# The gathered rows of expert 1: turned on the TensorE, with its weights issued from ScalarE's queue

## The chip, the cores and the metric

The kernel runs on one core of one Trainium2 chip. The metric is the device time of one execution in microseconds (us). The kernel before was timed three times: 347.15, 348.68 and 349.33 us, median 348.68 us. A fourth execution was recorded by the hardware profiler; all times inside the program come from it.

The core has five engines with a queue of instructions each: the TensorE (PE in the profile, its weight loads PEld), VectorE (DVE), ScalarE (ACT), GpSimd (POOL) and SyncE (SP). DMAs are issued from the queues of SP, ACT and POOL, and each engine carries out its own queue in order.

## The reference: what is computed

Two layers follow one another. The first is an mLSTM cell over 4 sequences, 8 heads, 768 steps and heads of 40, which gives a row of 320 numbers for each of the 3072 tokens. The second sends each token to one of eight experts by its id and applies that expert's two matrices:

```python
expert_idx = token_ids * np.int64(2654435761) % np.int64(E)      # E = 8
for e in range(E):
    mask = expert_idx == e
    xe = x[mask]                                                  # some 384 rows of 320
    h = np.maximum(xe @ w1[e], 0.0)                               # w1[e]: 320 x 1024
    out[mask] = h @ w2[e]                                         # w2[e]: 1024 x 320
```

All of it is fp32.

## The kernel before

**First half.** The sequence is cut into 24 pieces of 128 steps, which are worked through one after the other (the loop at L877). The rows that come out are stored to `x_rows` in DRAM. Beside this the routing is worked out: `g_idx` holds for each expert the numbers of its rows in `x_rows`, `s_idx` where the results go. Near the end of this half, 256 rows of expert 0 are gathered, turned on the TensorE (`early_turn`, L782) and put through layer 1 (L985), since they come from pieces that are done early.

**An expert's rows.** Each expert has CAP = 416 places: NJ = 3 blocks of 128 rows and RM = 32 more. The 32 of four experts are gathered together in one block of 128 (`xr0` for experts 0 to 3). Layer 1 needs the rows turned: `xT` has the 320 features along the partitions, as three blocks of 128, the third of which has only 64 features and carries them twice, for a product that uses both halves of the array. A row block is gathered by an indirect DMA from POOL (`gather`, L111).

There are two ways from gathered rows to `xT`:

- By way of slots in DRAM (experts 1 to 7): `fetch(e)` (L1198) gathers three blocks into `xg` and stores them to `x_slots` (L1206), `blocks(e)` (L1215) reads them back with 12 DMAs in pieces of 32 features, 128 bytes each, and `turned(e)` (L1223) turns all 32 x 32 squares with one VectorE instruction (L1225). The stores and the reads are issued by SP, and each waits for the one before it to land.
- On the TensorE (the rest of expert 0): `turn` (L1010) makes two transposes into PSUM, copies the last 64 features beside themselves on VectorE (L1015), makes the third transpose (L1016) and copies the result to `xT` on VectorE (L1020) or ScalarE (L1018). `turn_third` does so for the third block of expert 0, `turn_rest` for `xr0`, of which only the first 32 columns, those of expert 0, are kept.

**An expert's products.** Expert 0 uses plain products (`layer1`, L144, and `layer2`, L1122). Experts 1 to 7 use a scheme of seven products of half size in place of eight (`layer1_by_seven`, `layer2_by_seven`); it needs sums of blocks of the weights and of the rows beforehand: `sums_of_w1` (four VectorE instructions, L1029 to L1032) gives `sw`, `sums_of_x` (four, L1036 to L1039) gives `tx`, `differences_of_w2` (four on GpSimd) gives `tw`. The first product of an expert needs `w1t` and `xT`; the second needs `sw` and `tx`. The third row block and the 32 rows use plain products.

**Weights.** `weights` (L92) issues four DMAs: `w1t` (1024 KB, L98), `w1c` in two of 128 KB each (L101) and `w2t` (1280 KB, L103). In PSUM, `psum()` hands out eight banks in turn.

**The order of the work.** The program's text fixes each engine's order. After the first half it reads: `fetch(0)` (the third block of expert 0 and `xr0`, and the store of `xr0` to the slots, L1213); the first three weight DMAs of expert 1; `fetch(1)`; `blocks(1)`; expert 1's `w2t`; then in the loop (L1246) for expert 0 `fetch(2)`, `blocks(2)`, the weights of expert 2, and its products: layer 2 of two row blocks with `turn_third` after the first and `turn_rest` inside the second, a scatter of each to the output (a copy from PSUM on ScalarE, L997, and an indirect DMA of POOL, L1001), layer 1 of the remaining 160 rows, `sums_of_w1`, `turned(1)`, `sums_of_x`, and layer 2 of the third block. All these weights are issued by SP, so that expert 1's stand in one queue with the stores and reads of the slots.

Of the kernel before, what the change touches and what calls it, by code (L numbers as in the profile page):

```python
# [9 lines left out]
F32 = mybir.dt.float32  # L10
# [8 lines left out]
P = 128  # L19
# [4 lines left out]
def kernel(  # L24
# [24 lines left out]
    nc = tc.nc  # L49
# [4 lines left out]
    Dm = H * D  # L54
    E, _, F = moe_w1.shape
# [9 lines left out]
    DB = len(dch)  # L65

    NJ = 3
    RM = 32
    EG = P // RM
    NM = NJ * P  # L70
    CAP = NM + RM
# [17 lines left out]
    s_idx = consts.tile([P, NC], I32, name="s_idx")  # L89
    xe = consts.tile([1, NX + 1], I32, name="xe")  # L90

    def weights(src1, src2, wpool, w2pool, eng=None, meanwhile=lambda: None):  # L92

        eng = eng or nc.sync
        w1t = wpool.tile([P, 2, F], F32, name="w1t")
        w1c = wpool.tile([P, FB // 2, P], F32, name="w1c")
        w2t = w2pool.tile([P, FB, Dm], F32, name="w2t")
        eng.dma_start(w1t[:], src1[: 2 * P, :].rearrange("(a p) f -> p a f", p=P))  # L98
        last = src1[2 * P :, :].rearrange("d (a two f) -> two d a f", two=2, f=P)
        for i in range(2):  # L100
            eng.dma_start(w1c[i * P // 2 : (i + 1) * P // 2], last[i])  # L101
        meanwhile()
        eng.dma_start(w2t[:], src2.rearrange("(a p) d -> p a d", p=P))  # L103
        return w1t, w1c, w2t

# [5 lines left out]
    def gather(xg, idx, rows=N):  # L111
        nc.gpsimd.indirect_dma_start(  # L112
            out=xg, out_offset=None, in_=x_d[:rows, :], in_offset=bass.IndirectOffsetOnAxis(ap=idx, axis=0),
        )

    W = {}

    def load_weights(e, *args):

        W[e] = weights(moe_w1[e], moe_w2[e], wpools[e % 3 > 0], w2pools[e % 6 > 0], None, *args)  # L120

    def slices_of(e):

# [72 lines left out]
    with tc.tile_pool(name="gates", bufs=1) as gp, \  # L196
# [189 lines left out]
        def turn(s, what, tag="tr"):  # L386
            turned_in(s, what, tag)
            turned_out(s, what)
# [618 lines left out]
            tc.declare_no_dep(ins, group="rows_out", reason="disjoint rows")  # L1007
            tc.add_to_no_dep_group("rows_out", ins)

    def turn(xg, dst, on_act, n=P):  # L1010

        tp = psum().rearrange("p (d c) -> p d c", c=P)[:, :DB]
        for db in range(2):
            nc.tensor.transpose(tp[:, db, :], xg[:, db * P : (db + 1) * P], ident[:])
        nc.vector.tensor_copy(xg[:, Dm:], xg[:, 2 * P : Dm])  # L1015
        nc.tensor.transpose(tp[:, 2, :], xg[:, 2 * P :], ident[:])  # L1016
        if on_act:
            nc.scalar.copy(dst, tp[:, :, :n])  # L1018
        else:
            nc.vector.tensor_copy(dst, tp[:, :, :n])  # L1020

    def bank(i):
        return psum()[:, :CAP]
# [98 lines left out]
    def layer2(w, h, js, idx, apart, between=lambda j: None, within=lambda j, fb: None):  # L1122
        for j in js:
            zp = psum()[:, :Dm]
            for fb in range(FB):
                nc.tensor.matmul(  # L1126
                    zp, lhsT=h[:, fb, j * P : (j + 1) * P], rhs=w[2][:, fb, :],
                    start=(fb == 0), stop=(fb == FB - 1),
                )
                within(j, fb)  # L1130
            scatter(zp, idx(j), apart)
            between(j)
# [57 lines left out]
    def cols_of(t, c0):  # L1190
        return lambda j: t[:, c0 + j : c0 + j + 1]

    with tc.manual_schedule():
        xTs, hrem, xbs = {}, {}, {}
        xr0 = xp.tile([P, DB * P], F32, name="xr0", bufs=1)
        xTs[0] = xT0

        def fetch(e):  # L1198
            if e == 0:
                gather(xg0[:, 2, :Dm], cols_of(g_idx, 0)(2))  # L1200
                gather(xr0[:, :Dm], cols_of(g_idx, NR)(0))
            else:
                xg = xp.tile([P, NJ, Dm], F32, name="xg")
                for j in range(NJ):
                    gather(xg[:, j], cols_of(g_idx, e * NJ)(j))
                nc.sync.dma_start(xs_d[e, :NM].rearrange("(t p) d -> p t d", p=P), xg[:])  # L1206
            if e % EG == 0:
                if e:
                    xr = xp.tile([P, Dm], F32, name="xrg", bufs=1)
                    gather(xr[:], cols_of(g_idx, NR + e // EG)(0))  # L1210
                else:
                    xr = xr0[:, :Dm]
                nc.sync.dma_start(xs_d[e : e + EG, NM:], xr[:])  # L1213

        def blocks(e):  # L1215
            xb = xbs[e] = xp.tile([P, CAP // 32, DB, 32], F32, name="xb")
            rows = xs_d[e].rearrange("(g j) d -> j g d", j=32)
            for q in range(4):
                for c in range(DB):
                    d0 = c * P + (q if c + 1 < DB else q % 2) * 32  # L1220
                    nc.sync.dma_start(xb[q * 32 : (q + 1) * 32, :, c], rows[:, :, d0 : d0 + 32])  # L1221

        def turned(e):  # L1223
            xT = xTs[e] = xp.tile([P, DB, CAP], F32, name="xT")
            nc.vector.transpose(xT.rearrange("p c (g j) -> p g c j", j=32), xbs.pop(e)[:])  # L1225

        def turn_third():
            turn(xg0[:, 2], xT0[:, :, 2 * P : NM], False)

        def turn_rest():  # L1230
            turn(xr0, xT0[:, :, NM:], True, RM)

        def rest(g):
            zp = psum()[:, :Dm]
            for fb in range(FB):
                for i in range(EG):
                    nc.tensor.matmul(  # L1237
                        zp[i * RM : (i + 1) * RM, :], lhsT=hrem[g][:, i, fb, :], rhs=W[g * EG + i][2][:, fb, :],
                        start=(fb == 0), stop=(fb == FB - 1),
                    )  # L1240
            scatter(zp, cols_of(s_idx, NR + g)(0), True)

        fetch(0)
        load_weights(1, lambda: (fetch(1), blocks(1)))
        h = h0
        for e in range(E):  # L1246
            g, i = e // EG, e % EG
            if e + 2 < E:
                fetch(e + 2)
                blocks(e + 2)  # L1250
                load_weights(e + 2)
            if i == 0:
                hrem[g] = xp.tile([P, EG, FB, RM], F32, name="hrem")
            if e == 0:
                layer2(W[0], h, range(2), cols_of(s_idx, 0), True, lambda j: j == 0 and turn_third(), lambda j, fb: (j, fb) == (1, FB - 3) and turn_rest())
                layer1(W[0], xT0, h, 2 * P, CAP, bank)
                sw = sums_of_w1(W[1])
                turned(1)
                tx = sums_of_x(xTs[1])
            else:  # L1260
                tw = differences_of_w2(W[e])
                sh = xp.tile([P, 4, FB // 2, P], F32, name="sh", bufs=1)
                layer1_by_seven(
                    W[e], sw, xTs[e], tx, h, lambda: 2 < e < E - 1 and turned(e + 1),
                    lambda g: sums_of_h(h, sh, g, nc.vector if g else nc.gpsimd),
                )
            nc.gpsimd.tensor_copy(hrem[g][:, i], h[:, :, NM:])
            layer2(W[e], h, (2,), cols_of(s_idx, e * NJ), True)
            if 0 < e < E - 1:
                sw = sums_of_w1(W[e + 1])  # L1270
            if i == EG - 1 and e + 1 < E:
                rest(g)
            if e + 1 == E:
                nc.gpsimd.drain()
            if e > 0:
                txs = []

                def meanwhile():
                    if e < 3:
                        turned(e + 1)  # L1280
                    if e + 1 < E:
                        txs.append(sums_of_x(xTs[e + 1]))

                layer2_by_seven(W[e], tw, h, sh, cols_of(s_idx, e * NJ), meanwhile)
                tx = txs[0] if txs else None
            if e + 1 == E:
                rest(g)
    nx = nc.values_load(xe[0:1, NX : NX + 1], min_val=0, max_val=NX)
    with tc.If(nx > 0):
        with tc.For_i(0, nx, 1) as k:  # L1290
            ex = nc.sync.value_load(xe[0:1, bass.ds(k, 1)], min_val=0, max_val=E - 1)
            gs = xp.tile([P, 2], I32, name="gs")
            nc.vector.tensor_copy(gs[:, 0:1], g_idx[:, bass.ds(k + (NC - NX), 1)])
            nc.vector.tensor_copy(gs[:, 1:2], s_idx[:, bass.ds(k + (NC - NX), 1)])
            w = weights(
                moe_w1[bass.ds(ex, 1)].rearrange("e d f -> (e d) f"),
                moe_w2[bass.ds(ex, 1)].rearrange("e f d -> (e f) d"), wpools[0], w2pools[0],
            )
            xr = xp.tile([P, DB * P], F32, name="xr0", bufs=1)
            xT = xp.tile([P, DB, CAP], F32, name="xT")  # L1300
            gather(xr[:, :Dm], gs[:, 0:1])
            turn(xr, xT[:, :, :P], False)
            layer1(w, xT, h0, 0, P, bank)
            layer2(w, h0, range(1), lambda j: gs[:, 1:2], False)

# [29 lines left out]
```

## Time and profile before

| what | us |
|---|---|
| median of three runs | 348.68 |
| the three runs | 347.15, 348.68, 349.33 |
| the profiled execution | 349.48 |
| its span, first to last instruction | 347.7 |
| TensorE busy in it | 326.8 |
| expert 0's second part begins (layer 2 of the first block) | 133.62 |
| expert 1's first product begins | 158.86 |

The profiled execution is 1.78 us longer than its span, which is what lies before the first and after the last instruction, and 0.80 us longer than the median. In rows of the timeline the columns are the start in us from the span's beginning, the time it took, the engine, the line, the operation, what it writes and reads, how many are merged in the row, and in brackets how long the engine was idle before and what ended that. SPq, ACTq and POOLq are issues of DMAs: their time is that of the issue, not of the transfer.

### The profile page before, as it was taken

Reading aid. Unit: us, or ns where it says so; the run is one execution under the profiler, and the core shown is the slowest. Engines: PE = TensorE matmul, PEld = TensorE weight load, DVE = VectorE, ACT = ScalarE, POOL = GpSimd, SP = SyncE. Lnnn points to the kernel's source line nnn. Section 1 sums busy time; section 2 is a strip of 40 time slices with the busy share of each in tenths; the row PEclk is TensorE's granted clock in tenths of the full one; section 3 lists DMA queues with packets and bytes.
Section 4 is the critical chain, followed back from the end, with each engine's and each line's share of the span. In section 5 each row is a group of like instructions: output and inputs, shape, how many; then the busy total and the mean of one; then the engine's idle time right before and its main releaser. Section 6 shows DMA issues by size and latency. Waiting matters only on the chain.

```text
span 347.7 us, 10269 instructions
## 1 busy us (share of the span) xinstructions
PE 326.8 (94%) x4059; PEld 289.8 (83%) x4059; DVE 225.3 (65%) x526; ACT 131.7 (38%) x342; POOL 207.0 (60%) x325
## 2 busy tenths in 40 slices
PE   8889979999988799797999999999999999999994
PEld 8668879999977687567899899889989889899892
DVE  7698978888878641046676696834785775764610
ACT  4777567777756421111511411411411501511510
POOL 7795579898753416417625956933954946627613
PEclk9999999999999999999999999999999999999998
DMA  6997989998799984948596967959579478001001
GB/s 125 171 192 131 178 151 162 192 190 181 150 229 219 239 297 90 311 88 286 84 340 142 260 224 175 326 101 289 179 132 310 123 175 240 2 18 41 1 20 41
DMA packets 161977, 59.12 MB, mean 170 GB/s; under 512 B 140389, under 2 KB 157409, under 8 KB 161897
## 3 DMA queue, kind: packets, MB, share of 16 engines
q1 hardware_dynamic: 156694, 47.47, 59.3%
q0 software_dynamic: 3168, 10.49, 9.3%
q8 instruction: 33, 0.54, 0.7%
q10 hardware_dynamic: 2064, 0.48, 0.6%
q14 instruction: 18, 0.14, 0.1%
HBM read 46.25 MB, written 12.33 MB: 168 GB/s over the span
## 4 chain that ended last, share of the span: by engine, by line
PE 72%; DMA 8%; DVE 7%; issue 4%; SPq 3%; POOL 3%; ACT 2%; POOLq 0%; DVEq 0%; ACTq 0%
PE mh L1075 20%; PE mh L1159 15%; PE mh L1126 9%; PE mh L1083 6%; DMA v<-in_v_dram 5%; PE xh L534 5%; PE tr L397 4%; PE sp L461 3%; PE mh L160 2%; DMA x_slots<-xg 2%; DVE w L477 2%; SPq L1221 1%; PE mh L1237 1%; PE ab L420 1%; PE tr L513 1%
## 5 line engine op out<-in xcount | busy, mean ns | idle before, releaser
L1001 POOL DMA_INDIRECT out_dram<-zo,s_idx x26 | 26.5, 1020 | 69.9 <-issue 41.2
L1126 PE MATMUL mh<-w2t,h 128*128 128x320 f32 x160 | 44.9, 432 | 0.0
L1126 PEld LDWEIGHTS mh<-w2t,h 128*128 128x128 f32 x160 | 30.1, 190 | 11.0
L1061 DVE TENSOR_TENSOR h<-u,mh 128x416 f32<-128x416 f32 (+1 forms) x56 | 25.4, 475 | 16.5 <-PE mh L1083 8.4
L112 POOL DMA_INDIRECT xg<-x_rows,g_idx x24 | 23.5, 978 | 16.1 <-issue 6.7
L1075 PE MATMUL mh<-tx,sw 128*128 128x208 f32 x168 | 31.9, 340 | 0.0
L1075 PEld LDWEIGHTS mh<-tx,sw 128*128 128x128 f32 x168 | 29.7, 190 | 0.2 <-DVE tx L1037 0.2
L477 DVE TENSOR_TENSOR w<-sp,w 128x384 f32<-128x384 f32 x48 | 24.4, 550 | 7.0 <-ACT w L424 7.0
L1061 DVE TENSOR_TENSOR u<-m,mh 128x416 f32<-128x416 f32 x28 | 16.5, 588 | 18.8 <-PE mh L1075 15.6
L1159 PE MATMUL mh<-tw,sh 128*128 128x160 f32 x168 | 27.4, 299 | 0.0
L461 PE MATMUL sp<-qT,kT 64*64 64x64 f32 (+1 forms) x960 | 23.7, 233 | 2.8 <-DVE w L477 2.7
L1075 PE MATMUL mh<-xT,w1t 128*128 128x208 f32 x112 | 23.2, 340 | 3.2 <-DVE xT L1225 3.2
L461 PEld LDWEIGHTS sp<-qT,kT 64*64 64x64 f32 x960 | 19.8, 134 | 7.3 <-issue 4.6
L534 PE MATMUL xh<-v,w 128*64 128x41 f32 x384 | 25.9, 228 | 0.0
L534 PEld LDWEIGHTS xh<-v,w 128*64 128x64 f32 x384 | 24.5, 138 | 0.0
L1159 PEld LDWEIGHTS mh<-tw,sh 128*128 128x128 f32 x168 | 24.3, 190 | 0.0
L1075 PEld LDWEIGHTS mh<-xT,w1t 128*128 128x128 f32 x112 | 19.7, 190 | 3.7 <-DVE xT L1225 3.7
L1089 ACT COPY m<-mh 128x416 f32<-128x416 f32 x14 | 7.1, 507 | 40.7 <-PE mh L1075 31.5
L424 ACT ACTIVATE w<-ab 128x384 f32<-128x384 f32 x48 | 21.1, 484 | 2.6 <-PE ab L423 2.4
L1083 PE MATMUL mh<-xT,w1c 64*128 64x208 f32 x224 | 21.6, 342 | 0.0
L1159 PE MATMUL mh<-w2t,h 128*128 128x160 f32 x112 | 21.0, 300 | 0.0
L1083 PEld LDWEIGHTS mh<-xT,w1c 64*128 64x128 f32 x224 | 19.3, 187 | 1.8 <-issue 1.8
(276 smaller groups left out, 826.1 us busy)
## 6 DMA issues: line engine op xcount, KB each, us to landing
w2t<-in_moe_w_dram SPq DMA_DIRECT2D x7, 1280.0 KB
w1t<-in_moe_w_dram SPq DMA_DIRECT2D x7, 1024.0 KB
xb<-x_slots SPq DMA_DIRECT2D x84, 52.0 KB
k<-in_k_dram SPq DMA_DIRECT2D x24, 160.0 KB
v<-in_v_dram SPq DMA_DIRECT2D x24, 160.0 KB
og<-in_o_gate_dram SPq DMA_DIRECT2D x24, 160.0 KB
q<-in_q_dram SPq DMA_DIRECT2D x23, 160.0 KB
x_slots<-xg SPq DMA_DIRECT2D x7, 480.0 KB
```

What stands on the lines that cost most here:

```text
L112: nc.gpsimd.indirect_dma_start(out=xg, out_offset=None, in_=x_d[:rows, :], in_offset=bass.IndirectOffsetOnAxis(ap=idx, axis=0),)
L397: nc.tensor.transpose(tp[:, j, :], d[what][:, 2 * j : 2 * j + 2, :].rearrange("p h d -> p (h d)"), ident[:])
L424: nc.scalar.activation(w[:, hf], ab, AF.Exp)
L461: nc.tensor.matmul(sp[hf][o * HB : (o + 1) * HB, m, bs], lhsT=kT[r, 2 * m + j, i], rhs=qT[r, 2 * m + j, ts], start=True, stop=True,)
L477: nc.vector.tensor_tensor(d["w"][:, hf], d["sp"][hf], d["w"][:, hf], op=ALU.mult)
L534: nc.tensor.matmul(xh[half[i], hs], lhsT=lhsT, rhs=rhs, start=first[i], stop=last, skip_group_check=True)
L1001: ins = nc.gpsimd.indirect_dma_start(out=out[:, :], out_offset=bass.IndirectOffsetOnAxis(ap=idx, axis=0), in_=zo[:], in_offset=None, bound ...
L1061: nc.vector.tensor_tensor(o, a, b, op=ALU.add)
L1075: nc.tensor.matmul(pair(bank[n])[:, a], lhsT=lhsT(g + a), rhs=rhs, start=first and a == 0, stop=True, skip_group_check=True,)
L1083: nc.tensor.matmul(pair(bank[n])[:, a], lhsT=w1c[k, g + a, :], rhs=xT[k, 2, r], start=False, stop=True, skip_group_check=True,)
L1126: nc.tensor.matmul(zp, lhsT=h[:, fb, j * P : (j + 1) * P], rhs=w[2][:, fb, :], start=(fb == 0), stop=(fb == FB - 1),)
L1159: nc.tensor.matmul(bank[n], lhsT=lhsT(f), rhs=rhs(f), start=first and f == 0, stop=f == FB // 2 - 1, skip_group_check=True,)
```

## The change

Three things change, all around expert 1:

1. `fetch(1)` gathers its three blocks into a new tile `xg1` that has room for the doubled features, and no longer stores them to the slots; `blocks(1)` and `turned(1)` are gone. Instead `turn_second(j)` turns each block on the TensorE after expert 0's layer 1; the copies from PSUM go to VectorE, ScalarE and VectorE.
2. `turn_rest` also copies columns 32 to 64 of the turned `xr0` block, which are expert 1's 32 rows, to its `xT`.
3. Expert 1's weights are issued from ScalarE's queue, after ScalarE's copies for the two scatters of expert 0. `fetch(2)`, `blocks(2)` and expert 2's weights come behind the two scatters too, and no longer ahead of them.

```diff
-    def weights(src1, src2, wpool, w2pool, eng=None, meanwhile=lambda: None):
+    def weights(src1, src2, wpool, w2pool, eng=None):
...
-        meanwhile()
         eng.dma_start(w2t[:], src2.rearrange("(a p) d -> p a d", p=P))
...
-    def load_weights(e, *args):
+    def load_weights(e, eng=None):
 
-        W[e] = weights(moe_w1[e], moe_w2[e], wpools[e % 3 > 0], w2pools[e % 6 > 0], None, *args)
+        W[e] = weights(moe_w1[e], moe_w2[e], wpools[e % 3 > 0], w2pools[e % 6 > 0], eng)
...
-    def turn(xg, dst, on_act, n=P):
+    def turn(xg, *dsts):
...
         nc.tensor.transpose(tp[:, 2, :], xg[:, 2 * P :], ident[:])
-        if on_act:
-            nc.scalar.copy(dst, tp[:, :, :n])
-        else:
-            nc.vector.tensor_copy(dst, tp[:, :, :n])
+        for i, (copy, dst) in enumerate(dsts):
+            n = dst.shape[-1]
+            copy(dst, tp[:, :, i * n : (i + 1) * n])
...
+        xg1 = xp.tile([P, NJ, DB * P], F32, name="xg1", bufs=1)
...
         def fetch(e):
...
+            elif e == 1:
+                for j in range(NJ):
+                    gather(xg1[:, j, :Dm], cols_of(g_idx, NJ)(j))
...
         def turn_rest():
-            turn(xr0, xT0[:, :, NM:], True, RM)
+            xTs[1] = xp.tile([P, DB, CAP], F32, name="xT")
+            turn(xr0, (nc.scalar.copy, xT0[:, :, NM:]), (nc.vector.tensor_copy, xTs[1][:, :, NM:]))
+
+        def turn_second(j):
+            turn(xg1[:, j], ((nc.vector.tensor_copy, nc.scalar.copy)[j % 2], xTs[1][:, :, j * P : (j + 1) * P]))
...
         fetch(0)
-        load_weights(1, lambda: (fetch(1), blocks(1)))
+        fetch(1)
         h = h0
         for e in range(E):
             g, i = e // EG, e % EG
-            if e + 2 < E:
+            if 0 < e < E - 2:
                 fetch(e + 2)
                 blocks(e + 2)
                 load_weights(e + 2)
...
                 layer2(W[0], h, range(2), cols_of(s_idx, 0), True, lambda j: j == 0 and turn_third(), lambda j, fb: (j, fb) == (1, FB - 3) and turn_rest())
+                load_weights(1, nc.scalar)
+                fetch(2)
+                blocks(2)
+                load_weights(2)
                 layer1(W[0], xT0, h, 2 * P, CAP, bank)
+                for j in range(NJ):
+                    turn_second(j)
                 sw = sums_of_w1(W[1])
-                turned(1)
                 tx = sums_of_x(xTs[1])
```

More of the change, by code (lines that the diff above doesn't have):

```diff
@@ L1227, in turn_third @@
         def turn_third():
-            turn(xg0[:, 2], xT0[:, :, 2 * P : NM], False)
+            turn(xg0[:, 2], (nc.vector.tensor_copy, xT0[:, :, 2 * P : NM]))
         def turn_rest():
-            turn(xr0, xT0[:, :, NM:], True, RM)
+            xTs[1] = xp.tile([P, DB, CAP], F32, name="xT")
+            turn(xr0, (nc.scalar.copy, xT0[:, :, NM:]), (nc.vector.tensor_copy, xTs[1][:, :, NM:]))
+        def turn_second(j):
+            turn(xg1[:, j], ((nc.vector.tensor_copy, nc.scalar.copy)[j % 2], xTs[1][:, :, j * P : (j + 1) * P]))
         def rest(g):
@@ L1301 @@
             gather(xr[:, :Dm], gs[:, 0:1])
-            turn(xr, xT[:, :, :P], False)
+            turn(xr, (nc.vector.tensor_copy, xT[:, :, :P]))
             layer1(w, xT, h0, 0, P, bank)
```

## The prediction, made before the changed kernel was run

> **What bounds the kernel now.** I read the page first, for the engine that carries the span and where it is not full:
>
> ```profile
> span 347.7 us, 10269 instructions
> PE 326.8 (94%) x4059; PEld 289.8 (83%) x4059; DVE 225.3 (65%) x526; ACT 131.7 (38%) x342; POOL 207.0 (60%) x325
> ```
>
> The TensorE has work for 326.8 of 347.7 us. What a change around expert 1 can give is the idle time of PE there, so the second view is busy time by stretches: expert 0's layer 2, its layer 1, the hand-over to expert 1, expert 1, and the rest.
>
> ```profile
> core 0: us, PE busy (x) PEld busy (x) DVE busy (x) ACT busy (x) POOL busy (x), PEclk, DMA share, GB/s
> 133.60:144.80 11.20, 9.46 (x39) 6.45 (x37) 1.68 (x5) 1.01 (x4) 7.00 (x8) 1.00 0.78 223
> 144.80:151.20 6.40, 6.31 (x48) 5.63 (x49) 1.29 (x5) 1.28 (x5) 1.00 (x1) 1.00 0.55 178
> 151.20:158.80 7.60, 4.50 (x18) 2.88 (x16) 4.13 (x6) 0.73 (x2) 2.86 (x3) 1.00 0.72 133
> 158.80:184.00 25.20, 25.14 (x160) 23.20 (x161) 16.95 (x35) 6.46 (x15) 12.77 (x12) 1.00 0.80 236
> 184.00:338.50 154.50, 154.50 (x1025) 142.33 (x1024) 97.42 (x185) 38.47 (x91) 91.41 (x86) 1.00 0.56 153
> ```
>
> From 158.8 to 338.5 PE is never idle (154.50 of 154.50 us) and its clock is granted in full. So the end follows from when expert 1's first product starts: a microsecond won or lost there arrives whole, and nothing later can be won. Before it lie two holes, which PE's timeline names:
>
> ```profile
> 141.49 0.38 PE L1014 MATMUL mh<-ident,xr 128*128 128x128 f32 x2
> 141.71 0.27 PE L1016 MATMUL mh<-ident,xr 128*128 128x128 f32 x1
> 141.82 1.24 PE L1126 MATMUL mh<-w2t,h 128*128 128x320 f32 x4
> 144.89 1.35 PE L160 MATMUL mh<-xT,w1t 128*128 128x160 f32 x8 [1.83 <-ACT xT L1018]
> 151.23 4.47 PE L1126 MATMUL mh<-w2t,h 128*128 128x320 f32 x16
> 158.86 0.97 PE L1075 MATMUL mh<-xT,w1t 128*128 128x208 f32 x4 [3.17 <-DVE xT L1225]
> 159.69 0.62 PE L1075 MATMUL mh<-tx,sw 128*128 128x208 f32 x2
> ```
>
> The large hole, 3.17 us, waits for expert 1's turned rows, and the timeline shows why they are late:
>
> ```profile
> 137.29 0.42 SPq L98 DMA_DIRECT2D w1t<-in_moe_w_dram  x1
> 143.04 0.38 SPq L1206 DMA_DIRECT2D x_slots<-xg  x1
> 149.44 6.02 SPq L1221 DMA_DIRECT2D xb<-x_slots  x12
> 157.33 1.48 DVE L1225 STREAM_TRANSPOSE xT<-xb 128x1248 f32<-128x1248 f32 x1 [3.40 <-DMA xb<-x_slots]
> 159.25 0.38 DVE L1037 TENSOR_TENSOR tx<-xT,tx 128x208 f32<-128x208 f32 x1
> ```
>
> The store of the gathered rows (143.04) takes until 149.44 to land, the twelve reads take 6.02 us to issue and 1.9 more to land. That chain of 15.8 us is what the change takes out.
>
> The small hole is odd. The transposes of `xr` end at 141.71 + 0.27 = 141.98, but the ScalarE copy that frees PE starts only at 144.60:
>
> ```profile
> 144.60 0.24 ACT L1018 COPY xT<-mh 128x96 f32<-128x96 f32 x1 [6.00 <-remote]
> 144.74 0.43 ACT L997 COPY zo<-mh 128x320 f32<-128x320 f32 x1
> 131.54 1.01 POOL L112 DMA_INDIRECT xg<-x_rows,g_idx  x1 [4.80 <-PE mh L153]
> 140.44 0.96 POOL L112 DMA_INDIRECT xg<-x_rows,g_idx  x1 [0.30 <-issue]
> 141.70 1.03 POOL L1001 DMA_INDIRECT out_dram<-zo,s_idx  x1 [0.30 <-issue]
> ...
> 166.21 3.08 PE L1083 MATMUL mh<-xT,w1c 64*128 64x208 f32 x32
> 167.22 0.52 ACT L1100 ACTIVATE h<-mh 128x416 f32<-128x416 f32 x1 [3.16 <-PE mh L1083]
> 191.18 3.08 PE L1083 MATMUL mh<-xT,w1c 64*128 64x208 f32 x32
> 191.79 0.95 POOL L112 DMA_INDIRECT xrg<-x_rows,g_idx  x1 [0.30 <-issue]
> 194.00 0.52 ACT L1100 ACTIVATE h<-mh 128x416 f32<-128x416 f32 x1 [4.97 <-PE mh L1083]
> ```
>
> From 131.54 to 142.73 POOL issues nine indirect DMAs back to back, and ScalarE hears of PE's work 1.9 us after the last. The same happens in expert 2: the copy at L1100 comes 1.01 us after its products start in expert 1 (167.22 against 166.21), but 2.82 us after in expert 2 (194.00 against 191.18), 1.3 us after the last gather of another such train (192.74). I read it so: during a long train of indirect DMAs, ScalarE hears late of PE's results. This is an inference from two places.
>
> **The small hole.** After the change, POOL's first train is five gathers, as before until 137.6, and the first scatter, whose ScalarE copy is done at 138.6:
>
> ```profile
> 138.17 0.43 ACT L997 COPY zo<-mh 128x320 f32<-128x320 f32 x1 [3.96 <-DMA xg<-x_rows,g_idx]
> ```
>
> It ends near 139.7; `fetch(2)` now stands behind the second scatter. With 1.9 us after 139.7 the notice is back by 141.6, before the transposes end at 141.98. Then L1018 runs at once and PE goes on to layer 1 when the last matmuls of layer 2 allow, at about 142.9 (a PE group begins some 0.16 us before the recorded end of the one before). Gain 144.89 - 142.9 = 2.0 us. Its bounds are 0, if the hole has another cause, and 2.0.
>
> **The turns that are added.** Nine transposes stand between layer 1 and the third block's layer 2. One issues 0.11 us after the other (141.49 to 141.71 for two), 1.0 us in all; but each turn's third transpose waits for VectorE's copy of 64 features. Rows for the durations:
>
> ```profile
> 134.47 0.20 DVE L1015 COPY xg<-xg 128x64 f32<-128x64 f32 x1 [5.80 <-DMA xg<-x_rows,g_idx]
> 138.46 0.56 DVE L1020 COPY xT<-mh 128x384 f32<-128x384 f32 x1 [3.13 <-PE mh L1126]
> 150.88 0.33 DVE L167 TENSOR_SCALAR h<-mh 128x160 f32<-128x160 f32 x1 [0.69 <-PE mh L160]
> 151.12 0.68 DVE L1029 TENSOR_TENSOR sw<-w1t 128x512 f32<-128x512 f32 x1
> 153.24 0.69 DVE L1032 TENSOR_TENSOR sw<-w1t,sw 128x512 f32<-128x512 f32 x1
> ```
>
> On the old clock: VectorE's last relu ends at 151.21; copy of the features to 151.45; third transpose to 151.82; copy of block 0 out of PSUM (0.56) to 152.41; the features of block 1 to 152.65, its transpose, and ScalarE copies it to 153.6; the features of block 2 to 152.9, its transposes to 153.2, copied by 153.9. PE starts layer 2 at about 153.15 instead of 151.23: 1.92 us lost. The lower bound is the 1.0 us of issue; the upper is three turns in which PE waits for the copy of 0.56 each time, 2.8 us. I take 1.92, the order of the queues as written.
>
> [...]
>
> **The large hole.** PE is done with the third block's layer 2, so far as the next group may begin, at 155.53 on the old clock, and started expert 1 at 158.86. Of these 3.33 us all come back if `xT`, `w1t`, `sw` and `tx` are ready. With the new start (2.0 earlier, 1.92 later) the first product is due at 155.46 and the second, 0.83 us on (159.69 - 158.86), at 156.3. VectorE is free of copies at 153.9 - 2.0 = 151.9. The four `sw` took 151.12 to 153.93, 2.8 us, so 154.7; the second of four `tx` at 0.39 each, 155.5. That is in time, if `w1t` is there at 151.9.
>
> **The weights on ScalarE.** These rows of expert 2 give the issues and the transfer:
>
> ```profile
> 172.08 0.47 SPq L98 DMA_DIRECT2D w1t<-in_moe_w_dram  x1
> 172.60 1.19 SPq L101 DMA_DIRECT2D w1c<-in_moe_w_dram  x2
> 173.84 0.60 SPq L103 DMA_DIRECT2D w2t<-in_moe_w_dram  x1
> 177.55 0.69 DVE L1029 TENSOR_TENSOR sw<-w1t 128x512 f32<-128x512 f32 x1 [1.95 <-DMA w1t<-in_moe_w_dram]
> ```
>
> The second scatter's copy is done at about 143.55, so ScalarE issues from 143.6 to 145.9 (2.3 us). Queued behind them is the first relu of layer 1, due 1.1 us earlier; it catches up by the third, and PE does not wait, since layer 1 fills other banks. `w1t` took 5.5 us in expert 2 and lands at 149.1. For the upper bound, let one scatter and three gathers of 160 KB each go first: 1664 KB at the 178 GB/s of the stretch from 144.8 take 9.6 us, `w1t` lands at 153.2, and the second `tx` at 156.8, 0.5 us late for the second product. Between 0 and 0.5 I take 0.2, nearer to the row of expert 2, because the slot traffic of expert 1 is gone from this stretch.
>
> **Moved without cost.** SP is free of expert 1: expert 2's store goes out when its gathers land, no longer behind expert 1's reads, and its weights follow sooner than at 172.08, where `sw` waited 1.95 us for them under cover of PE's work. On POOL the gathers of expert 2 move behind both scatters; next in its queue is the copy of the 32 rows' hidden values, due only after the last relu, 151.21 - 2.0. The copy of expert 1's 32 rows out of `turn_rest` falls where VectorE is idle. If that cover were gone it would cost its 0.24 us.
>
> **Sum.** Minus 2.0, plus 1.92, minus 3.33, plus 0.2: 3.2 us less. The span of 347.7 becomes 344.5, its execution (1.78 around it) 346.3; the profiled execution was 0.80 above the median of the runs, so 345.5.
>
> **Rivals.**
>
> *The small hole stays*, because it is not POOL's train that makes it; or the timed runs never had it, and nothing can be won there. For it: only two places bear my reading, and the cause of the wait is not named (`remote`). Against it: both waits end soon after a train's end. Then 3.33 - 1.92 = 1.4 us are won: 347.3.
>
> *The late notice moves.* The second scatter and three gathers now run from 143.6 to about 148.6, under layer 1. If ScalarE and VectorE hear late until some 150.2, the last relu, due at 148.9, comes some 1.3 us late, and the features' copies with it: 1.9 us won, 346.8. For it: a train with PE at work. Against it: four are fewer than nine.
>
> *Slower: expert 1's weights come late.* They now start some 6 to 8 us later than 137.29. Break-even is `w1t` landing at 156.1: then `sw` and two of `tx` end at 159.7, when the second product started before. If all 2560 KB must come for the last of `w1t` to be in, at the 223 GB/s of the stretch from 133.6, that is 11.8 us; with the small hole left (issue at 145.2) it lands at 157.0, 0.9 us too late: 349.6. Each microsecond more costs one. [...] Against it is expert 2's row, with 5.5 us while a second weight matrix was behind it.
>
> **How the numbers follow.** Forecast 0.45, small hole stays 0.30, notice moves 0.15, weights late 0.06, something else 0.04. The likeliest gives 345.5, alone from 344.6 (turns at 1.0 us) to 346.5 (turns at 2.8). The range reaches to 348.2, over the two middle rivals and the spread of the runs shown. About 1% is what a measurement of this kernel can tell from no change: 345.2 is the line. Half of the forecast's chance lies near or under it, and little of the rest: 0.25 faster, 0.73 within, 0.02 slower, as even late weights stay within 1%.
>
> **What would show it.** In the new profile: ScalarE's L1018 copy near 142 and layer 1 from 142.9; three turns after 149, with 1.9 us between layer 1 and the third block; expert 1's first product near 155.5 without a wait; no idle PE after it. Wrong: L1018 still past 144; PE waiting for `w1t` or `sw`; an added hole in experts 2 to 7, which I give no price.

## The result, and the profile after

The changed kernel took 342.83 us in the median of four runs (342.30 to 343.73); the kernel before took 348.51 us beside it, also in four. The ratio is 0.9843, 95% interval 0.9804 to 0.9883: 5.7 us less, where 3.2 were forecast and 344.6 was the lower end of the range. The profiled execution took 342.30 us, span 340.5. Medians here and below are of all runs; ratios and their intervals leave out those more than 1.5% above the fastest of the same kernel. First the page: PE has nine matmuls more, the transposes, and 326.4 us of work for 326.8, so nothing was saved in the products and the 7 us of the span were idle time.

```profile
span 340.5 us, 10272 instructions
...
PE 326.4 (96%) x4068; PEld 289.3 (85%) x4068; DVE 225.4 (66%) x531; ACT 132.5 (39%) x343; POOL 206.0 (61%) x325
```

Busy time by stretches, cut as in the prediction: expert 0's layer 2, its layer 1, the hand-over, expert 1, the rest.

```profile
core 0: us, PE busy (x) PEld busy (x) DVE busy (x) ACT busy (x) POOL busy (x), PEclk, DMA share, GB/s
130.40:139.70 9.30, 9.30 (x40) 6.65 (x39) 1.86 (x6) 1.05 (x3) 4.35 (x5) 1.00 0.44 122
139.70:145.90 6.20, 6.20 (x49) 5.51 (x48) 1.29 (x5) 1.33 (x4) 3.90 (x4) 1.00 0.80 249
145.90:152.00 6.10, 5.57 (x28) 4.06 (x27) 4.90 (x14) 0.78 (x2) 0.39 (x1) 1.00 0.92 303
152.00:177.00 25.00, 25.00 (x162) 23.23 (x161) 16.06 (x32) 6.87 (x16) 14.76 (x14) 1.00 0.80 213
177.00:331.30 154.30, 154.30 (x1024) 141.64 (x1023) 97.11 (x184) 38.98 (x91) 91.21 (x86) 1.00 0.54 151
```

PE is idle in one of them only, for 0.53 us. Its timeline, in the rows that answer to those of before (L1013 and L1015 are the transposes, L159 is layer 1 of expert 0, L1124 layer 2, L1073 expert 1's first products):

```profile
138.51 0.27 PE L1015 MATMUL mh<-ident,xr 128*128 128x128 f32 x1
138.62 1.24 PE L1124 MATMUL mh<-w2t,h 128*128 128x320 f32 x4
139.69 1.25 PE L159 MATMUL mh<-xT,w1t 128*128 128x160 f32 x8
...
144.73 1.35 PE L159 MATMUL mh<-xT,w1t 128*128 128x160 f32 x8
145.93 0.38 PE L1013 MATMUL mh<-ident,xg 128*128 128x128 f32 x2
...
147.17 0.33 PE L1015 MATMUL mh<-ident,xg 128*128 128x128 f32 x1 [0.53 <-DVE xg L1014]
...
147.66 4.47 PE L1124 MATMUL mh<-w2t,h 128*128 128x320 f32 x16
151.97 0.87 PE L1073 MATMUL mh<-xT,w1t 128*128 128x208 f32 x4
152.67 2.27 PE L1073 MATMUL mh<-tx,sw 128*128 128x208 f32 x12
```

Both holes are gone: layer 1 starts 0.91 us after the transposes end, and expert 1's first product follows the third block's layer 2 with no wait. ScalarE and VectorE around it:

```profile
138.82 0.24 ACT L1018 COPY xT<-mh 128x96 f32<-128x96 f32 x1 [3.42 <-PE mh L1015]
...
139.90 0.38 ACTq L98 DMA_DIRECT2D w1t<-in_moe_w_dram  x1
140.32 1.28 ACTq L101 DMA_DIRECT2D w1c<-in_moe_w_dram  x2
141.64 0.61 ACTq L102 DMA_DIRECT2D w2t<-in_moe_w_dram  x1
142.30 0.30 ACT L168 ACTIVATE h<-mh 128x160 f32<-128x160 f32 x1 [1.98 <-PE mh L152]
```

```profile
148.34 0.68 DVE L1027 TENSOR_TENSOR sw<-w1t 128x512 f32<-128x512 f32 x1
```

The weights take 2.35 us of issue. The first relu comes 2.61 us after layer 1's start, where the second profile of the kernel before (experiment 1) has 1.80, so it is 0.8 us late, and PE does not notice. `sw` starts with no idle time ahead of it, so `w1t` was there.

**The changed half was forecast well.** This execution began expert 0's layer 2 at 130.42 where the profile of before had 133.62. Put back by these 3.20 us, the marks are: L1018 at 142.02 (forecast "near 142"), layer 1 at 142.89 (142.9), expert 1 at 155.17 (near 155.5, without a wait). What was wrong is not what the change does, but what it was compared with.

### The profile page after: what moved, and what is told of

It is laid out like the page before. It is cut to its first block, busy times and chain, and to the rows that moved or that the text cites. A ratio compares the mean times of both kernels' runs of the same rounds, so it can differ in the third digit from the quotient of the medians.

```text
span 340.5 us, 10272 instructions
## 1 busy us (share of the span) xinstructions
PE 326.4 (96%) x4068; PEld 289.3 (85%) x4068; DVE 225.4 (66%) x531; ACT 132.5 (39%) x343; POOL 206.0 (61%) x325
## 4 chain that ended last, share of the span: by engine, by line
PE 80%; DMA 7%; POOL 3%; DVE 3%; issue 3%; ACT 2%; SPq 1%; POOLq 0%; ACTq 0%; DVEq 0%
PE mh L1073 21%; PE mh L1157 16%; PE mh L1124 13%; PE mh L1081 6%; PE xh L533 5%; DMA v<-in_v_dram 4%; PE tr L396 4%; PE sp L460 4%; PE mh L159 4%; DMA q<-in_q_dram 2%; DMA xg<-x_rows,g_idx 1%; PE mh L1243 1%; PE ab L419 1%; PE mh L152 1%; PE tr L512 1%
## 5 line engine op out<-in xcount | busy, mean ns | idle before, releaser
L1000 POOL DMA_INDIRECT out_dram<-zo,s_idx x26 | 26.5, 1017 | 74.1 <-issue 40.2
L1124 PE MATMUL mh<-w2t,h 128*128 128x320 f32 x160 | 44.9, 432 | 0.0
L1124 PEld LDWEIGHTS mh<-w2t,h 128*128 128x128 f32 x160 | 30.1, 190 | 11.0
L1073 PE MATMUL mh<-tx,sw 128*128 128x208 f32 x168 | 31.8, 339 | 0.0
L1073 PEld LDWEIGHTS mh<-tx,sw 128*128 128x128 f32 x168 | 29.7, 190 | 0.0
L533 PE MATMUL xh<-v,w 128*64 128x41 f32 x384 | 25.9, 228 | 0.0
L1073 PE MATMUL mh<-xT,w1t 128*128 128x208 f32 x112 | 23.1, 339 | 0.0
L996 ACT COPY zo<-mh 128x320 f32<-128x320 f32 x12 | 5.1, 425 | 42.1 <-PE mh L1124 27.7
```

The source lines that it names most:

```text
L533: nc.tensor.matmul(xh[half[i], hs], lhsT=lhsT, rhs=rhs, start=first[i], stop=last, skip_group_check=True)
L1000: ins = nc.gpsimd.indirect_dma_start(out=out[:, :], out_offset=bass.IndirectOffsetOnAxis(ap=idx, axis=0), in_=zo[:], in_offset=None, bound ...
L1073: nc.tensor.matmul(pair(bank[n])[:, a], lhsT=lhsT(g + a), rhs=rhs, start=first and a == 0, stop=True, skip_group_check=True,)
L1124: nc.tensor.matmul(zp, lhsT=h[:, fb, j * P : (j + 1) * P], rhs=w[2][:, fb, :], start=(fb == 0), stop=(fb == FB - 1),)
```

## The experiments

**1. The kernel before, profiled a second time**, no edit.

> The kernel before, unchanged, for a second profile. Two marks are read in every run here: when expert 0's layer 2 starts on the TensorE (133.62 us in the kernel before, 130.42 in the changed one, though no instruction ahead of it differs), and the stretch from there to expert 1's first product (25.24 and 21.55 us). If the first mark moves by itself from one execution to the next, it comes out anywhere from 130 to 134 here. If the change made it earlier, it is 133 to 134 again. The stretch should be 25.2 again, with the hole of 1.8 us at the copy of the 32 rows if that hole belongs to the kernel, and 23.4 without it if it was a chance of the one profile.

Measured: 346.93 us, span 345.1. Expert 0's layer 2 starts at 127.89 and the PE timeline reads:

```profile
137.16 1.25 PE L160 MATMUL mh<-xT,w1t 128*128 128x160 f32 x8
...
143.39 4.47 PE L1126 MATMUL mh<-w2t,h 128*128 128x320 f32 x16
153.51 1.76 PE L1075 MATMUL mh<-xT,w1t 128*128 128x208 f32 x4 [5.65 <-DVE xT L1225]
155.06 4.37 PE L1075 MATMUL mh<-tx,sw 128*128 128x208 f32 x12
```

The small hole is absent, the large one is 5.65 us in one piece, and behind it the twelve products with `sw` take 4.37 us where the changed kernel has 2.27. Three stretches of the same profile say why:

```profile
core 0: us, PE busy (x) PEld busy (x) DVE busy (x) ACT busy (x) POOL busy (x), PEclk, DMA share, GB/s
145.90:152.70 6.80, 1.96 (x8) 1.06 (x6) 0.93 (x2) 0.42 (x1) 3.18 (x4) 1.00 0.73 147
152.70:159.50 6.80, 5.99 (x17) 5.84 (x18) 3.28 (x8) 0.51 (x1) 2.71 (x3) 0.50 0.82 286
159.50:166.30 6.80, 6.80 (x54) 6.54 (x55) 3.05 (x6) 1.76 (x4) 4.11 (x3) 1.00 0.52 82
```

PEclk is 0.50 for 6.8 us. Some 6.0 us of PE's work fall into that and cost 3.0 us more than at full clock. From expert 1's first product to the end it is 191.62 us here, against 188.81 in the first profile of before and 188.52 in the changed kernel.

And the small hole: the same train of nine indirect DMAs is there, without it (GpSimd's first and eighth, then ScalarE's copy, the transposes having ended at 136.25):

```profile
125.58 1.01 POOL L112 DMA_INDIRECT xg<-x_rows,g_idx  x1 [4.58 <-DMA x_rows<-x]
...
134.47 0.95 POOL L112 DMA_INDIRECT xg<-x_rows,g_idx  x1 [0.30 <-issue]
```

```profile
136.28 0.24 ACT L1018 COPY xT<-mh 128x96 f32<-128x96 f32 x1 [3.42 <-PE mh L1016]
```

The second place that the prediction leaned on, expert 2, is ordinary here too: the copy comes 1.06 us after its products' start, with the train still there.

```profile
188.68 3.08 PE L1083 MATMUL mh<-xT,w1c 64*128 64x208 f32 x32
```

```profile
189.74 0.52 ACT L1100 ACTIVATE h<-mh 128x416 f32<-128x416 f32 x1 [3.22 <-PE mh L1083]
```

So the train does not by itself delay the notice (it is also whole in experiment 2, without the delay), and removing the delay moves idle time rather than taking it out: expert 1 starts when the slots are through, whether PE waits once or twice on the way (1.83 + 3.17 = 5.00 us of idle then, 5.65 now). The theory from here on: the change wins the slots' hole in every execution, and on top of it about 3 us of half clock in those executions in which the hole is long and in one piece. The rival: the extra gain comes from the moved queue, or from chance in the first half.

**2. The turns alone.** The changed kernel with expert 1's weights, `fetch(2)`, `blocks(2)` and expert 2's weights ahead of layer 2, on SyncE, as before the change.

```diff
         fetch(0)
+        load_weights(1)
         fetch(1)
+        fetch(2)
+        blocks(2)
+        load_weights(2)
...
-                load_weights(1, nc.scalar)
-                fetch(2)
-                blocks(2)
-                load_weights(2)
```

> Expert 1's rows are turned on the TensorE as in the change, but its weights are issued by SyncE right after the first gathers, and expert 2's gathers, slots and weights come ahead of expert 0's layer 2, as before. GpSimd again has eight gathers and a scatter back to back. If the long train makes ScalarE hear late, the hole of 1.5 to 2 us before layer 1 is there, and the stretch is 21.55 + 1.8 = 23.3 us; the time 1.5 to 2 us above the changed kernel. If the hole needs the slot traffic of expert 1, it is gone and the stretch is 21.5.

Measured: 343.07 us beside 347.54, ratio 0.9894 (0.9808 to 0.9981). In its profile the stretch from expert 0's layer 2 to expert 1's first product is 21.55 us and the rest 188.56, to 0.04 us those of the changed kernel. The turns carry the whole gain that can be seen; the place of the weights gives nothing by itself.

**3. The queue alone.** The kernel before, slots kept, with expert 1's weights on ScalarE behind the two scatters and expert 2's work behind them.

```diff
-        load_weights(1, lambda: (fetch(1), blocks(1)))
+        fetch(1)
+        blocks(1)
...
-            if e + 2 < E:
+            if 0 < e < E - 2:
...
+                load_weights(1, nc.scalar)
+                fetch(2)
+                blocks(2)
+                load_weights(2)
```

> The other half alone: expert 1's rows go by way of the slots, as before, but its weights are issued from ScalarE behind the two copies for the scatters, and expert 2's gathers, slots and weights come behind too. By the theory of two holes, the small hole is gone (train of five gathers and a scatter), the store of the rows goes out at about 140 on the old clock instead of 143, lands without the weights beside it in some 4 us, and the twelve reads take 6 + 2 us, so the rows are turned at about 153.5 and expert 1 starts near 154: a stretch of 20.5 to 21.5 us with no TensorE work added, a time like the changed kernel's or 1 us below. If the turning on the TensorE is what the gain comes from, the reads now compete with the weights and the stretch stays at 23.5 to 25.

Measured: 347.76 us, ratio 1.0001 (0.9952 to 1.0051). No gain, but a stall of another kind. ScalarE, PE and SyncE:

```profile
141.30 0.41 ACTq L98 DMA_DIRECT2D w1t<-in_moe_w_dram  x1
149.96 1.27 ACTq L101 DMA_DIRECT2D w1c<-in_moe_w_dram  x2
...
152.15 0.89 ACT L168 ACTIVATE h<-mh 128x160 f32<-128x160 f32 x4 [11.65 <-DMA xb<-x_slots]
```

```profile
152.51 6.72 PE L1125 MATMUL mh<-w2t,h 128*128 128x320 f32 x14 [5.70 <-ACT h L168]
```

```profile
141.34 10.74 SPq L1220 DMA_DIRECT2D xb<-x_slots  x12
```

ScalarE issues `w1t` and then stands for 8.25 us ahead of `w1c`, which goes out at 149.96. The four relus behind it come at 152.15, and the view puts the end of ScalarE's 11.65 us without work down to a slot read of SyncE. Why the one stands behind the other is an inference from other profiles: in the records of those of before and of the changed kernel the DMAs of SyncE and ScalarE, 260 and 247 of them, signal on the same eight semaphores, in 251 of 259 and 235 of 246 steps on the next one in turn, and each of the two `w1c` DMAs of the changed kernel (140.32 and 140.98) waits on the one that it will signal itself. So `w1c` is taken here to have waited for a semaphore that a slot read still held. PE waits 5.70 us for the relus, and 6.8 us at half clock follow (PEclk 0.50 from 151.10 to 157.90).

**4. Only the gathers ahead.** The changed kernel with `fetch(2)` ahead of layer 2, to restore the long train and look for the small hole.

```diff
         fetch(1)
+        fetch(2)
...
                 load_weights(1, nc.scalar)
-                fetch(2)
                 blocks(2)
```

> The changed kernel with one call moved: the three gathers of expert 2 (and the store of their rows) come ahead of expert 0's layer 2 again, so that GpSimd issues eight gathers and a scatter back to back; the weights stay on ScalarE, behind. If the long train makes the late notice, ScalarE's copy of the 32 rows starts some 1 to 2 us after the train's end, the hole of 1.5 to 2 us is back and the stretch 23.2 us or more. If the transfer of weights during the gathers made it, there is no hole and the stretch is 21.5.

Measured: 348.09 us, ratio 1.0039 (0.9996 to 1.0083): the whole gain gone, though by neither theory. The small hole does not come back (L1018 at 136.85, transposes' end 136.82), but the stall of experiment 3 does:

```profile
147.14 1.63 ACTq L101 DMA_DIRECT2D w1c<-in_moe_w_dram  x2
...
149.47 0.89 ACT L168 ACTIVATE h<-mh 128x160 f32<-128x160 f32 x4 [11.11 <-DMA xb<-x_slots]
```

```profile
149.83 0.69 PE L1013 MATMUL mh<-ident,xg 128*128 128x128 f32 x2 [5.37 <-ACT h L168]
```

**5. The same with the weights on SyncE**, to see whether ScalarE's queue is the cause.

```diff
-                load_weights(1, nc.scalar)
+                load_weights(1)
```

> The variant with expert 2's gathers ahead, where ScalarE stood 9 us in the issue of expert 1's second weight DMA, with the one difference that SyncE issues these weights, at the same place of the program. If the queue of ScalarE is what made the hole (its relus wait behind a DMA that waits for a completion semaphore that the slot reads hold), the hole is gone: stretch 21.5 us, time 342 to 343.5. If the transfers themselves collide, the stretch stays near 29 and the time at 348.

Measured: 341.48 us beside 347.85, ratio 0.9839 (0.9747 to 0.9931). The gain is back, and the view of waits has one row for PE after 120 us, the changed kernel's own (who waits, for whom; us in total, times, longest):

```profile
PE mh L1015 <- DVE xg L1014: 0.5, 1, 0.5
```

The DMAs in ScalarE's queue are harmless in the changed kernel: their last issue ends at 142.25, and its slot reads come only from 153.62 on, so there is none that they could stand behind.

**6. The hole filled.** The kernel before with 18 products of the identity behind expert 0's third block, which nothing reads. Expert 1 starts no sooner by it; only PE is kept at work.

```diff
             layer2(W[e], h, (2,), cols_of(s_idx, e * NJ), True)
+            if e == 0:
+                t = psum()
+                for _ in range(18):
+                    nc.tensor.matmul(t[:, :P], lhsT=ident[:], rhs=ident[:], start=True, stop=True)
```

> The kernel before with 18 products of the identity with itself on the TensorE, whose result nobody reads, between the third block's layer 2 and expert 1. Nothing gets earlier; the TensorE only has work in the hole in which it waits for the turned rows. The second profile of the kernel before had one hole of 5.65 us and then 6.8 us of half clock, and 191.6 us from expert 1's start to the end, against 188.5 in the changed kernel. If the half clock is a price of the hole, the clock stays full here, the last stretch is 188.5 to 188.8, the stretch before it stays at 25.2 to 25.9, and the median is 2 to 3 us below the kernel before. If the half clock has another cause, or costs nothing because the matmuls wait for other engines anyway, the time is that of the kernel before or above.

Measured: 345.42 us beside 347.85, ratio 0.9941 (0.9897 to 0.9986). Work was added and the kernel became faster (the rows count two matmuls to an unread product):

```profile
148.62 4.18 PE L1272 MATMUL mh<-ident 128*128 128x128 f32 x36
152.69 0.97 PE L1075 MATMUL mh<-xT,w1t 128*128 128x208 f32 x4
153.51 2.38 PE L1075 MATMUL mh<-tx,sw 128*128 128x208 f32 x12
```

The twelve products take 2.38 us instead of 4.37, and the granted clock is 0.990 or less in one of ten runs, against ten of thirteen of the kernel before beside it. The price of the half clock, 2.4 us in the medians (0.5 to 3.6 by the ratio's interval), is thereby measured without any of the change's parts. Two marks of the profile are not as expected. From expert 1's first product to the end it is 189.80 us and not 188.5 to 188.8; 0.50 of this is a wait for GpSimd at 196.47, the rest has no cause named. And the stretch before it is 23.89 us and not 25.2 to 25.9: in this execution the rows were turned by 152.64, so expert 1 did start sooner. In the five profiles of before and of experiments 1, 6, 7 and 8, all with expert 1's rows in slots and its weights on SyncE, that stretch lies anywhere from 23.9 to 26.5 us, so a single profile cannot divide the gain.

**7. Half filled**: 9 products instead of 18.

> The kernel before with 9 unread products of the identity in the hole in place of 18, some 2 us of work, so that some 3.6 us of the 5.6 stay idle in one piece. If the clock falls only after an idle stretch well over 3.2 us in one piece (the profile of before kept full speed through 1.83 and 3.17 us), this half is as good as the whole: about 345.4 beside 347.8 for the kernel before, the clock from 0.993 up, no half speed after the hole. If idle time is priced by its length, half the gain: about 346.6, and the products behind the hole still at half speed in most executions.

Measured: 347.01 us beside 348.12, ratio 0.9947 (0.9894 to 1.0000), the granted clock at 0.990 or less in five of ten runs, against fifteen of sixteen of the kernel before. That is near the second expectation, half of the gain, but it does not decide for it: the hole had been assumed at 5.6 us in every execution, and in this profile it was 6.5 us, 2.0 of it filled, with half clock behind what was left (PEclk 0.50 from 155.20 to 162.00).

```profile
149.34 2.17 PE L1272 MATMUL mh<-ident 128*128 128x128 f32 x18
156.04 1.75 PE L1075 MATMUL mh<-xT,w1t 128*128 128x208 f32 x4 [4.54 <-DVE xT L1225]
```

That the clock fell behind 4.54 us of idle is new; the experiment does not tell pieces from totals.

**8. The hole split.** The same nine products, reading a part of `xb` that comes back late, so that they would stand between two pieces of idle.

```diff
-                    nc.tensor.matmul(t[:, :P], lhsT=ident[:], rhs=ident[:], start=True, stop=True)
+                    nc.tensor.matmul(t[:, :P], lhsT=ident[64:96, :], rhs=xb1[64:96, :4, 1, :], start=True, stop=True)
```

> The kernel before with the same number of unread products as the half-filled hole, nine, but made to read a part of the rows that comes back from the slots as the eighth of the twelve reads, so that they stand in the middle of the hole and cut what stays idle into two pieces of some 1.5 to 2.5 us. Expert 1 starts no sooner than before. [...] If the idle total counts, as in the half-filled hole: half of the runs at 0.990 or less. If the clock has nothing to do with the time: no change, 348.

Measured: 345.04 us, with 11 of 12 runs at a granted clock of 0.992 or more. That is the wholly filled hole's time and clock. But the kernel before, on this other chip, took 345.25 us, and the ratio is 0.9999 (0.9966 to 1.0033): here the clock held in 12 of its own 17 runs. The split can therefore not be credited by the ratio. Nor does the profile show one: the nine products follow the third block at 149.97 without a wait, so what they read was there by then, and 0.77 us are left idle behind them. What a hole in two pieces does was thus not measured. The profile shows another thing:

```profile
138.94 0.24 ACT L1018 COPY xT<-mh 128x96 f32<-128x96 f32 x1 [5.76 <-PE mh L1126]
```

```profile
139.23 1.35 PE L160 MATMUL mh<-xT,w1t 128*128 128x160 f32 x8 [1.59 <-ACT xT L1018]
...
149.97 2.27 PE L1273 MATMUL mh<-xb,ident 32*128 32x128 f32 x18
153.01 0.97 PE L1075 MATMUL mh<-xT,w1t 128*128 128x208 f32 x4 [0.77 <-DVE xT L1225]
```

The transposes had ended at 136.56, and the copy came 2.38 us later: the small hole of the first profile, once more. The late notice is real, then, but belongs to some executions and not to the kernel: of the fourteen profiles of this study two show it, this one and the first of before; of the twelve that do not, eight have the same train ahead of the copy. In the two, PE's signals to the other engines are recorded in bursts after gaps of 3 to 7 us, at several places each; the other twelve have none. Both kept full clock: PEclk is 1.00 from 133.60 to 338.50 in the first of before, and from 143.50 to 330.00 here.

**9. The copies early.** The turns alone (experiment 2), with the three copies of 64 features made ahead of expert 0's layer 1.

```diff
+                for j in range(NJ):
+                    nc.vector.tensor_copy(xg1[:, j, Dm:], xg1[:, j, 2 * P : Dm])
                 layer1(W[0], xT0, h, 2 * P, CAP, bank)
...
-            turn(xg1[:, j], ((nc.vector.tensor_copy, nc.scalar.copy)[j % 2], xTs[1][:, :, j * P : (j + 1) * P]))
+            turn(xg1[:, j], ((nc.vector.tensor_copy, nc.scalar.copy)[j % 2], xTs[1][:, :, j * P : (j + 1) * P]), doubled=True)
```

> The variant with the turns alone (weights on SyncE), with VectorE's three copies of 64 features moved ahead of expert 0's layer 1, so that no transpose waits for them. The nine transposes then issue in a row, 1.0 us instead of 1.7 between layer 1 and the third block; the stretch comes down from 21.55 to 20.8 us if the copy is the only thing that PE waits for there, and the time by 0.7. If VectorE's chain (two copies, four sums of weights, two of rows) becomes the bound, expert 1 waits for it and the stretch stays above 21.2.

> The version with the copies of the 64 features ahead of expert 0's layer 1 and the weights and gathers issued early, once more, beside the changed kernel on one chip. By the profiles its turns take 0.75 us less and the rest is alike, so 0.75 us under the changed kernel, about 0.2 %, which the scatter of the first half (several us between executions) may well hide.

It ran twice beside the changed kernel, which was expected as follows:

> The changed kernel, unchanged, on the chip of these runs. Stretch 21.55 us, 188.5 us from expert 1 to the end, no half clock in between; the start of expert 0's layer 2 anywhere between 127.9 and 133.6, as in the six profiles so far. Time 341 to 344. If the change itself made the first half earlier, that mark stays near 130.4.

> The changed kernel itself beside it: 341 to 343 us, ratio to the kernel before 0.984, stretch from expert 0's layer 2 to expert 1's first product 21.55 us, rest 188.5 us, no half speed.

Measured, first time: 341.28 us (ratio to before 0.9840, 0.9761 to 0.9920) beside 341.21 for the changed kernel (0.9838, 0.9761 to 0.9915); second time 340.70 (0.9815, 0.9760 to 0.9870) beside 342.17 (0.9868, 0.9817 to 0.9920). In the changed kernel's two profiles the stretch is 21.55 us and the rest 188.5, as expected, and expert 0's layer 2 begins at 127.80 and 129.41. Over both, the mean of ten runs is 0.89 us under that of eleven of the changed kernel, 95% interval 0.03 to 1.75. The hand-over in its profile, to be read against the third row of the changed kernel:

```profile
144.90:150.30 5.40, 5.40 (x28) 4.13 (x27) 4.65 (x11) 0.79 (x2) 0.40 (x1) 1.00 0.33 104
```

PE no longer waits at all, and the stretch to expert 1's first product is 20.80 us in both profiles instead of 21.55, so 0.75 us are there to be had. It is the best version of the study, by a margin that the runs only just show.

## Why the prediction was wrong

**The step that failed** stands under what bounds the kernel: "its clock is granted in full. So the end follows from when expert 1's first product starts: a microsecond won or lost there arrives whole, and nothing later can be won." That was true of the execution on the page and not of most. The kernel before has two kinds. Its 65 runs beside the experiments, all of them counted, divide by the granted clock of the whole span: 46 at 0.990 or less take 348.1 us on average, 19 above it take 345.0. The difference is 3.1 us (0.7 either way; on the three chips 2.2, 3.3 and 3.6), what the second profile shows as 191.62 - 188.52 = 3.10. The fifteen runs of the changed kernel average 342.0, and only one has a clock of 0.990 or less. In the fourteen profiles this limit does divide the kinds: the four with 6.8 us at half clock behind a hole have 0.983 to 0.990, the ten others 0.993 or more.

- Against the 19 runs that kept the clock, the change wins 3.0 us (0.75 either way; 12 of the 19 ran on the chip of experiment 8, where the changed kernel did not). The forecast was 3.2.
- Against the 46 others it wins 6.1 us, because it also removes the hole that costs them the clock. This term is missing from the sum.

Two profiles whose first halves end within 0.1 us of one another show both parts: the second one of before (layer 2 at 127.89) and the second of the changed kernel (127.80). The stretch falls from 25.62 to 21.55 us, 4.07; the rest from 191.62 to 188.52, 3.10; together 7.17 of the 7.25 us between the two executions.

The division by clock is a correlation over runs without a trace. What shows the cause are the traces with 6.8 us at half clock behind a hole (experiments 1, 3, 4, 7) and the filled hole (experiment 6), where the half clock goes though none of the change's parts is there. A low clock can have other causes too: three of the 18 runs of experiments 2, 5 and 9 have 0.990 or less without such a hole in their profiles.

**Point by point:**

- *The small hole, 2.0 us.* The copy did come at once in the changed kernel, but it does so without the change too, in four of the six profiles with expert 1's rows in slots. Where the delay exists it is not lost time, since PE would wait for the slots anyway. As a gain it should have been put together with the large hole: their sum is about 5 us in the first profile.
- *Rival 1, small hole gone in the timed runs, 347.3.* Its condition was true of most profiled executions, its price false for the same reason: without the small hole the large one grew to 5.65 us, so nothing of the 2.0 was lost to the change.
- *Turns, 1.92.* The nine transposes and their waits cost 1.74 us: from layer 1's last group at 144.73 to the third block at 147.66 it is 2.93 us, and in the second profile of before, without them, 1.19 (142.20 to 143.39). PE waits once for the copy of the features, 0.53 us, and the order of the queues was as foreseen.
- *Large hole, 3.33.* Gone, as forecast.
- *Weights, 0.2, and rival 3.* No wait for `w1t`. The range of 0 to 0.5 held at its lower end. The first relu was 0.8 us late where 1.1 were forecast.
- *Rival 2, the late notice moves.* Not seen in any of eight profiles of kernels with the turns.
- *The base.* The profiled execution was put 0.80 us above the median, and that was taken for a small shift of the whole. In fact two large differences nearly cancelled: its first half ended at 133.62, where thirteen other profiles have 127.80 to 130.60, and it had no half clock, 3.1 us. The sum was thus made in an execution that was slow where the change does nothing and quick where it does most.

How much idle time costs the clock, the traces show at the hole in single executions. Pieces of 1.83 and 3.17 us cost nothing in the first profile of before, where PEclk is 1.00 from 133.60 to 338.50; 4.54, 5.37, 5.65 and 5.70 us in one piece (experiments 7, 4, 1 and 3) each brought 6.8 us at PEclk 0.50, beginning 3.7 to 4.8 us into the hole. The profile of before had the two pieces some 11 us apart, and the prediction never asked what would follow if they came as one.

Elsewhere in the same traces the clock fell behind less. In the first half of experiment 6's profile, near 17 us, the clock is at half for 3.4 us, behind as long a stretch in which PE worked for 1.83 us and no idle piece was longer than 0.97 (columns as in the stretches above):

```profile
13.72:17.13 3.41, 1.83 (x28) 1.52 (x25) 2.33 (x7) 2.72 (x9) 3.09 (x14) 1.00 1.05 182
17.13:20.55 3.42, 3.42 (x61) 2.32 (x61) 3.39 (x4) 1.77 (x4) 3.28 (x8) 0.50 1.11 198
```

The profile of experiment 3 and the first of experiment 9 have the same there, behind 1.68 and 1.60 us of work. The first profile of before kept its clock over a stretch with no more work, the one that the large hole begins in:

```profile
154.12:157.53 3.41, 1.57 (x6) 0.76 (x4) 0.20 (x1) 0.43 (x1) 0.99 (x1) 1.00 0.69 102
157.53:160.95 3.42, 2.09 (x11) 1.92 (x12) 2.79 (x6) 0.51 (x1) 2.61 (x3) 1.00 0.96 297
```

So half clock also came behind short pieces that lie close together (0.97 us at most in experiment 6), and where the line runs these traces do not show. That two pieces of 1.83 and 3.17 us cost nothing is one execution, not a rule.

**What stays open.** Why PE's signals come late and in bursts in some executions, and whether the executions that keep the clock without a trace are those. That both traced cases kept it fits, but two are few. Why the clock fell behind half-idle stretches near 17 us and not behind others as idle. Also what moves the end of the first half, by 2.8 us over thirteen profiles and by 5.8 with the first, when its instructions are the same before and after the change.

## What to carry to other kernels

Two idle pieces on an engine that wait, in the end, for the same chain are one hole: add them, and ask what the engine's clock does if they come in one piece (here 5.65 us, with 6.8 us at half clock behind them) or close together. Profile the kernel before more than once, and compare its granted clock over the timed runs with that of the profile, before taking one execution for the kind that the median is made of. A DMA in the queue of a computing engine can hold that engine while other engines' DMAs run: ScalarE stood 8.25 and 8.76 us ahead of one, beside SyncE's slot reads (experiments 3 and 4).

## What the runs showed of the hardware that was not expected

- Eighteen products that nobody reads made a kernel 2.4 us faster (345.42 against 347.85, ratio 0.9941), by keeping PE at work through a hole.
- The clock fell to half for 3.4 us behind 3.41 us of half work, with no idle piece longer than 0.97 us (experiment 6, near 17 us).
- A DMA issue on ScalarE stood 8.25 and 8.76 us behind SyncE's slot reads (experiments 3 and 4), with `w1t` issued just ahead of it and ScalarE otherwise free. With the same DMAs on SyncE the ratio to the kernel before went from 1.0039 to 0.9839 (experiments 4 and 5).
- In two of fourteen profiled executions PE's signals reached the other engines up to 6.5 us late: in the first profile of before none of those due from 138.09 on is recorded ahead of 144.54, and ScalarE's copy starts at 144.60.
